# Later casts for the second expert, and other filler products on TensorE beside the first row gather

## The chip, the cores and the metric

The kernel runs on one core of a Trainium2 chip. The metric is the device time of one launch in microseconds (us). Three runs of the kernel before gave 1000.73, 1001.07 and 1002.69 us; their median is 1001.07 us. A difference is told from no change when it is over 0.2%, which is 2.0 us here.

## The reference

Attention over 48 pairs of batch and head with normalised queries and keys, then a mixture of eight experts with a fixed capacity of 224 tokens each, then one dense block with an ELU:

```python
def _moe_ref(x, w_gate, w1, w2):
    cap = N // E                      # 1792 // 8 = 224 tokens for each expert
    logits = x @ w_gate
    # tokens are given out greedily by logit, at most cap for each expert
    ...
    for e in range(E):
        mask = assigned == e
        h = np.maximum(x[mask] @ w1[e], 0.0)      # [224, 768] @ [768, 1024]
        out[mask] = h @ w2[e]                     # [224, 1024] @ [1024, 768]

def _moe2_ref(x, w_in, w_out):
    h = x @ w_in
    g = np.where(h > 0.0, h, np.exp(np.minimum(h, 0.0)) - 1.0)
    return (g @ w_out)
```

## The kernel before

The span has four parts: attention with the gate's logits (to about 300 us), the assignment of tokens to experts (to about 331 us), the eight experts (to about 570 us), and the dense block, whose second product is done by a scheme with seven products in place of eight (to the end). The change touches the seam between the assignment and the experts, from 331 us on. Experts are counted from 0 in the code, so "the second expert" is expert 1.

Every float32 operand of the experts is split into two float16 parts, a high one and a low one, and each product is the sum of three float16 products (high by high, high by low, low by high). For one expert the work is this:

- **Gather** (`Rows.gather`, line 875): two indirect DMAs, issued by GpSimd, fetch the expert's 224 rows as two halves `xg` of 112 rows. `gather(e + 2)` stands before the second products of expert `e`.
- **Columns** (`columns`, lines 906 to 924): ScalarE casts each half to float16 (`xh`, line 914), GpSimd subtracts for the low part (line 915; for expert 0 it is VectorE, in pieces of 256 columns), TensorE transposes both parts (`xt`, line 922; 24 products of 112 columns) and VectorE copies the result from PSUM to `xe` (line 923).
- **First products** (`ph`, line 951): eight tiles of 18 products, 224 columns each. For each tile ScalarE applies the ReLU and writes the high part of `h` (line 952), and VectorE the low part (line 953), which gives the PSUM bank back. Three banks serve `ph`.
- **Second products** (`py`, line 983): six tiles of 24 products; ScalarE and VectorE move each into `xc` (lines 933 and 934).
- **Weights**: SyncE loads each float32 tile into one of five staging buffers (`fw<-w`, line 810), ScalarE casts it (line 818), VectorE subtracts for the low part (line 820), and then the staging buffer is free for the next load. The first weights of expert 0 (`wa`) are made during the assignment, its second weights (`w2`, lines 802 and 806) between its `ph` tiles.

What sets the order: each engine runs its queue strictly in order. Blocks under `tc.manual_schedule()` keep the order of the code; elsewhere the order on each engine is made at build time by a scheduler that models the engines, and `tc.issue_after(x)` tells it to place instructions behind instruction `x`. The weights of expert 1 are placed behind the fourth ReLU of expert 0 in this way (`W.after`, lines 815 to 820). In the kernel before, `columns(1)` has no such condition, and the scheduler places its casts ahead of the ReLUs of expert 0 on ScalarE, and its first transposes inside the first `ph` tile on TensorE.

Between the end of the assignment and the arrival of expert 0's rows, TensorE runs 18 products into a bank nobody reads (line 940, tile `warm`). TensorE's clock has two granted levels, 1.2 and 2.4 GHz; the profile shows them as 0.50 and 1.00.

Of the kernel before, what the change touches and what calls it, by code (L numbers as in the profile page):

```python
# [20 lines left out]
P = 128  # L21
# [857 lines left out]
def moe(tc, xp, pre, xs, idx, idh, W, rows, ring, w1_d, w2_d, wi_d, wo_d, lin, g_d, t_d, out):  # L879
    nc = tc.nc  # L880
    with tc.tile_pool(name="mp", bufs=1, space=PSUM, reuse_waits="tile") as pp:
        bank = lambda t, name: pp.tile([P, 512], F32, tag=PS[t][0], name=name, bufs=PS[t][1])
# [8 lines left out]
        def wi_prep(f):  # L891

            for f in (f, f + 8):
                a = W.read64(wi_d[f], f"wi{f}")
                w = wic[f] = ring.tile([P, 2, 768], F16, tag="w1", name=f"wic{f}", bufs=8)
                nc.scalar.activation(w[:, 0], a, AF.Copy, scale=SW)
                nc.vector.scalar_tensor_tensor(w[:, 1], a, SW, w[:, 0], ALU.mult, ALU.subtract)
# [3 lines left out]
        with tc.tile_pool(name="m1", bufs=1, reuse_waits="tile") as sp:  # L901
            xe = {0: rows.first}

            def gather(e):
                xe[e] = rows.gather(e, [sp.tile([P, DM], F32, tag="xg", name=f"xg{e}_{h}", bufs=4) for h in range(2)])

            def columns(e):
                xg, x = xe[e], sp.tile([P, 6, 2, CAP], F16, tag="xe", name=f"xe{e}", bufs=2)
                hl = [sp.tile([P, 2, DM], F16, tag="xh", name=f"xh{e}_{h}", bufs=3) for h in range(2)]
                n = 256 if e == 0 else DM  # L910
                for h in (1, 0):
                    for a in range(0, DM, n):
                        x32, hi, lo = xg[h][0:112, a:a + n], hl[h][0:112, 0, a:a + n], hl[h][0:112, 1, a:a + n]
                        nc.scalar.activation(hi, x32, AF.Copy)  # L914
                        (nc.vector if e == 0 else nc.gpsimd).tensor_tensor(lo, x32, hi, ALU.subtract)  # L915
                xe[e] = x
                for d in range(0, 6, 2):
                    pt = bank(2 if e == 0 and d == 4 else 0, f"xt{e}_{d}").bitcast(F16)[:, 0:4 * CAP].rearrange("p (d j c) -> p d j c", d=2, j=2)
                    for k in range(2):
                        for h in (1, 0):  # L920
                            for j in range(2):
                                nc.tensor.transpose(pt[:, k, j, 112 * h:112 * h + 112], hl[h][0:112, j, (d + k) * P:(d + k + 1) * P], idh[0:112, 0:112])  # L922
                    last = nc.vector.tensor_copy(x[:, d:d + 2], pt)
                return last.ins

            def result(e, d, ps):

                ps = ps.rearrange("p (h c) -> p h c", h=2)
                for c, (a, b) in zip(xc, CB):
                    lo, hi = max(a, 112 * e), min(b, 112 * e + 112)  # L930
                    if lo < hi:
                        z, c = ps[:, :, lo - 112 * e:hi - 112 * e], c[:, :, d, :, lo - a:hi - a]
                        nc.scalar.activation(c[:, :, 0], z, AF.Copy, scale=SY)
                        nc.vector.scalar_tensor_tensor(c[:, :, 1], z, SY, c[:, :, 0], ALU.mult, ALU.subtract)

            with tc.manual_schedule():
                gather(1)
                warm = bank(2, "warm")
                for _ in range(18):
                    nc.tensor.matmul(warm, idh, W.ws[0].rearrange("p a b -> p (a b)")[:, 0:512], start=True, stop=True)  # L940
                W.after = columns(0)
                nc.vector.tensor_copy(ix2[0:112], idx[0:112])

                nc.scalar.dma_start(lin.rearrange("(h e r) -> r (h e)", h=2, e=E), ix2[0:112].rearrange("p h e -> p (h e)"))

                def first(e, f, w):
                    x, h = xe[e], hs[e]
                    ps = bank(1, f"ph{e}_{f}")[:, 0:CAP]
                    for d in range(6):
                        for n, (i, j) in enumerate(((0, 0), (0, 1), (1, 0))):  # L950
                            nc.tensor.matmul(ps, w[:, i, d * P:(d + 1) * P], x[:, d, j], start=d == 0 and n == 0, stop=d == 5 and n == 2)  # L951
                    relu = nc.scalar.activation(h[:, f, 0], ps, AF.Relu)
                    nc.vector.scalar_tensor_tensor(h[:, f, 1], ps, 0.0, h[:, f, 0], ALU.max, ALU.subtract)  # L953
                    return relu

                hs = {0: sp.tile([P, 8, 2, CAP], F16, tag="h", name="h0", bufs=2)}
                for f in range(8):
                    relu = first(0, f, W.ws[f])
                    if f == 3:
                        W.after = relu.ins  # L960
                    if f < 6:
                        if f >= 2:
                            W.second()
                        W.rest(f)
            nc.sync.dma_start(id2, lin.rearrange("(g p) -> p g", p=P))
            for e in range(E):
                if e:
                    hs[e] = sp.tile([P, 8, 2, CAP], F16, tag="h", name=f"h{e}", bufs=2)
                    for f in range(8):
                        first(e, f, W.split("w1", 8, w1_d[e, f], 768, f"w1_{e}_{f}"))  # L970
                h = hs[e]
                if e + 2 < E:
                    gather(e + 2)
                if e + 1 < E:
                    columns(e + 1)
                else:
                    wi_prep(0)
                for d in range(6):
                    w = W.split("w2", 6, w2_d[e, d], 1024, f"w2_{e}_{d}") if e else W.w2[d]
                    ps = bank(2, f"py{e}_{d}")[:, 0:CAP]  # L980
                    for f in range(8):
                        for n, (i, j) in enumerate(((0, 0), (0, 1), (1, 0))):
                            nc.tensor.matmul(ps, w[:, i, f * P:(f + 1) * P], h[:, f, j], start=f == 0 and n == 0, stop=f == 7 and n == 2)  # L983
                    result(e, d, ps)
        pre.close()
        with tc.tile_pool(name="wb", bufs=1, reuse_waits="tile") as wp:
# [64 lines left out]
            with tc.tile_pool(name="l1", bufs=1, side="right", reuse_waits="tile") as sp:  # L1051
# [21 lines left out]
                for f in range(8):  # L1073
# [10 lines left out]
                    if f == 7:  # L1084
                        first = operands(0, late)
# [80 lines left out]
```

## Time and profile before

| what | value |
|---|---|
| median of three runs | 1001.07 us |
| the profiled execution, its own time | 1000.04 us |
| its span, first to last instruction | 998.1 us |
| TensorE busy | 953.1 us (95%) |
| weight loads on TensorE | 629.7 us (63%) |
| VectorE busy | 754.9 us (76%) |
| ScalarE busy | 522.3 us (52%) |
| GpSimd busy | 287.1 us (29%) |
| mean granted TensorE clock | 0.985 |

The profiled execution took 1.9 us more than its span; that part lies around the program. TensorE is the busiest engine, but its share is an average: what a change at one place is worth is read from that place. Busy time of TensorE counts a product from its start to a modelled end, so products in a close row overlap in it; the distance from start to start is the price of one. "PEld" in the rows is TensorE's weight load, "SP" is SyncE, and "releaser" is what ended a wait.

### The profile page before, as it was taken

To read this page: it belongs to the slowest core of one execution; us is meant where nothing else is said; L and a number is where in the kernel's file an instruction comes from. 1 tells how busy PE (TensorE), PEld (TensorE's weight loads), DVE (VectorE), ACT (ScalarE), POOL (GpSimd) and SP (SyncE) were. 2 spreads that over 40 slices of the span, in tenths; PEclk is the share of its full clock that TensorE was granted. 3 is DMA by queue.
4 is the path that set the end of the run, shared out by engine and by line. 5 is a ranking of instruction groups with operands and counts; after the bars stand their busy time and mean duration, and the time that the engine had idled before them with its cause. 6 is when DMAs were issued, how large, how long until landed. Compare 5 with 4: busy or idle time off the path is not lost.

```text
span 998.1 us, 18586 instructions
## 1 busy us (share of the span) xinstructions
PE 953.1 (95%) x6922; PEld 629.7 (63%) x6922; DVE 754.9 (76%) x1424; ACT 522.3 (52%) x1148; POOL 287.1 (29%) x434
## 2 busy tenths in 40 slices
PE   5899999999998799999999999999999989999997
PEld 2445555555555499999999955555555546666664
DVE  6899999999958587877778699999924565555630
ACT  4778888888874276566664434334312233323330
POOL 5678888888721531121100000000000001000000
PEclk8999999999999799999999999999999999999999
DMA  9433434435215778877677168788674653333000
GB/s 336 164 104 117 127 118 123 145 115 148 56 39 177 188 205 265 263 240 225 207 236 247 38 232 266 236 284 253 209 241 122 201 151 107 100 112 115 34 32 32
DMA packets 100639, 164.92 MB, mean 165 GB/s; under 512 B 32960, under 2 KB 66240, under 8 KB 100160
## 3 DMA queue, kind: packets, MB, share of 16 engines
q1 hardware_dynamic: 96336, 152.66, 48.4%
q0 software_dynamic: 2400, 11.01, 3.6%
q8 instruction: 56, 0.92, 0.4%
q14 instruction: 39, 0.32, 0.1%
q10 hardware_dynamic: 1808, 0.01, 0.1%
HBM read 131.66 MB, written 31.99 MB: 164 GB/s over the span
## 4 chain that ended last, share of the span: by engine, by line
PE 58%; DMA 5%; DVE 1%; issue 1%; SPq 0%; ACT 0%; POOL 0%; POOLq 0%; ACTq 0%; DVEq 0%
PE l L1062 17%; PE ph L951 11%; PE py L983 11%; PE o_b L1101 10%; PE o_c L1101 6%; DMA g_d<-e 3%; PE o_a L1101 2%; PE xt L922 1%; DMA q<-g_d 1%; DMA xg<-xs,idx 1%; DVE e L1066 0%; DMA out<-xc,id 0%; DVE e L1065 0%; SPq L1022 0%; POOL xh L915 0%
## 5 line engine op out<-in xcount | busy, mean ns | idle before, releaser
L1062 PE MATMUL l<-xc,wic 128*128 128x384 f16 (+1 forms) x1152 | 218.2, 352 | 0.0
L1062 PEld LDWEIGHTS <-wic 128*128 128x128 f16 x1152 | 112.7, 98 | 104.8
L1101 PEld LDWEIGHTS <-a 128*128 128x128 f16 x1080 | 106.0, 98 | 75.3 <-ACT a L1038 3.9
L1117 POOL DMA_INDIRECT out<-xc,id x14 | 15.4, 1100 | 467.9 <-DVE xc L1110 441.8
L820 DVE SCALAR_TENSOR_TENSOR w<-fw,w 128x768 f16<-128x768 f32 (+1 forms) x98 | 110.0, 1127 | 25.9 <-ACT w L818 25.8
L244 ACT ACTIVATE p<-s,nb,r 128x448 f32<-128x448 f32 x144 | 104.0, 723 | 31.1 <-DVE nb L231 30.8
L983 PE MATMUL py<-h,w 128*128 128x224 f16 x1152 | 113.5, 259 | 0.0
L983 PEld LDWEIGHTS <-w 128*128 128x128 f16 x1152 | 109.8, 98 | 0.2
L225 DVE TENSOR_REDUCE nm<-s 128x1 f32<-128x448 f32 x168 | 102.9, 612 | 3.6 <-PE s L220 3.1
L951 PE MATMUL ph<-xe,w 128*128 128x224 f16 x1008 | 98.8, 259 | 1.4 <-DVE h L953 1.4
L951 PEld LDWEIGHTS <-w 128*128 128x128 f16 x1008 | 96.5, 98 | 1.6 <-issue 1.6
L1064 ACT ACTIVATE e<-l 128x512 f32<-128x512 f32 (+1 forms) x64 | 34.6, 541 | 113.8 <-PE l L1062 113.6
L818 ACT ACTIVATE w<-fw 128x768 f16<-128x768 f32 (+1 forms) x98 | 90.6, 928 | 5.9 <-DMA fw<-w 5.6
L282 ACT ACTIVATE e<-pt 128x448 f32<-128x448 f32 (+2 forms) x216 | 83.0, 422 | 12.3 <-PE pt L273 11.2
L297 PE MATMUL o<-e,v 128*64 128x448 f32 x384 | 87.8, 558 | 1.6 <-DVE xl L309 1.6
L273 PE MATMUL pt<-idn,p 128*128 128x128 f32 x432 | 71.4, 277 | 1.8 <-ACT p L244 1.4
L273 PEld LDWEIGHTS pt<-idn,p 128*128 128x128 f32 x432 | 50.6, 142 | 24.2 <-ACT e L282 13.2
L220 PE MATMUL s<-ks,qh 128*128 128x448 f16 x144 | 52.0, 361 | 12.5 <-ACT p L244 10.8
L915 POOL TENSOR_TENSOR xh<-xg,xh 112x768 f16<-112x768 f32 x14 | 24.3, 1755 | 129.8 <-ACT xh L914 129.8
L231 DVE TENSOR_TENSOR nb<-nm,r 128x1 f32<-128x1 f32 x168 | 59.4, 353 | 2.9
L1038 ACT ACTIVATE a<-s 128x1024 f16<-128x1024 f32 (+2 forms) x30 | 28.5, 966 | 55.8 <-PE o_b L1101 31.9
L1039 DVE SCALAR_TENSOR_TENSOR a<-s,a 128x1024 f16<-128x1024 f32 (+2 forms) x30 | 33.1, 1117 | 26.1 <-ACT a L1038 26.0
(244 smaller groups left out, 1668.0 us busy)
## 6 DMA issues: line engine op xcount, KB each, us to landing
fw<-w SPq DMA_DIRECT2D x56, 384.0 KB, 3.8
fw<-w SPq DMA_DIRECT2D x42, 512.0 KB, 4.5
xwi<-wi SPq DMA_DIRECT2D x16, 768.0 KB, 6.6
xwo<-wo SPq DMA_DIRECT2D x16, 768.0 KB, 5.1
q<-g_d SPq DMA_DIRECT2D x24, 512.0 KB, 3.7
qT<-qT SPq DMA_DIRECT2D x24, 448.0 KB, 4.2
qk<-qk SPq DMA_DIRECT2D x23, 448.0 KB, 3.5
g_d<-e SPq DMA_DIRECT2D x32, 256.0 KB, 4.4
```

Of the source, the lines that this page charges most:

```text
L225: nc.vector.tensor_reduce(d["nm", u], d["s", u][:, 0:448], AX.X, ALU.max, negate=True)
L231: nc.vector.tensor_tensor(d["nb", u], d["nm", u], d["r"][:, rc:rc + 1], ALU.mult)
L244: nc.scalar.activation(dst, d["s", u][:, 0:448], AF.Exp, bias=d["nb", u], scale=d["r"][:, rc:rc + 1], accum_out=d["sm"][:, rc:rc + 1])
L273: nc.tensor.transpose(pt[:, j * P:(j + 1) * P], p[j][:, h, 64 * h + c * P:64 * h + (c + 1) * P], idn)
L282: move = nc.vector.tensor_copy if u not in (0, 1, 2, 4, 5, 6) else lambda o, x: nc.scalar.activation(o, x, AF.Copy)
L297: nc.tensor.matmul(d["o"][64 * h:64 * h + 64, 0:448], d["v"][:, c + 4 * h, :], d["e", min(2 * c + h, 6)], start=c == 0, stop=c == 3)
L818: nc.scalar.activation(w[:, 0], f, AF.Copy, scale=SW)
L820: nc.vector.scalar_tensor_tensor(w[:, 1], f, SW, w[:, 0], ALU.mult, ALU.subtract)
L951: nc.tensor.matmul(ps, w[:, i, d * P:(d + 1) * P], x[:, d, j], start=d == 0 and n == 0, stop=d == 5 and n == 2)
L983: nc.tensor.matmul(ps, w[:, i, f * P:(f + 1) * P], h[:, f, j], start=f == 0 and n == 0, stop=f == 7 and n == 2)
L1062: nc.tensor.matmul(ps, w[:, i, d * P:(d + 1) * P], xc[cb][:, h, d, j], start=d == 0 and m == 0, stop=d == 5 and m == 2)
L1101: nc.tensor.matmul(ps, a[x][:, f, i], wt[b][f][:, j], start=first and f == 0 and k == 0, stop=f == 7 and k == 2, skip_group_check=True)
```

## The change

Two edits. The 18 filler products of 512 float16 columns become 46 others: 18 in float32 with 73 columns against 128 columns of weights, then ten pairs in float16 with 448 columns, each pair on the two halves of the array's rows (partitions 0 to 63 and 64 to 127, into two banks), then four pairs in float32 with 64 columns against 64 columns of weights on two quadrants. And `columns(1)` is placed behind the last product of the last `ph` tile of expert 0 (`mm.ins`) and behind its fifth ReLU (`relu4.ins`).

```diff
             with tc.manual_schedule():
                 gather(1)
-                warm = bank(2, "warm")
-                for _ in range(18):
-                    nc.tensor.matmul(warm, idh, W.ws[0].rearrange("p a b -> p (a b)")[:, 0:512], start=True, stop=True)
+
+                w0, w1, f0 = bank(2, "warm0"), bank(1, "warm1"), W.f2[0]
+                for k in range(18):
+                    nc.tensor.matmul(w0[:, 0:73], f0[:, k % 7 * P:(k % 7 + 1) * P], f0[:, 896:969], start=True, stop=True)
+                hl = W.ws[0].rearrange("p a b -> p (a b)")
+                for k in range(10):
+                    for r, w in ((0, w0), (64, w1)):
+                        nc.tensor.matmul(w[:, 0:448], hl[r:r + 64, k * P:(k + 1) * P], hl[r:r + 64, 0:448], start=True, stop=True)
+                for k in range(4):
+                    for r in (0, 64):
+                        nc.tensor.matmul(w0[r:r + 64, 0:64], f0[r:r + 64, k * 64:(k + 1) * 64], f0[r:r + 64, 896:960], start=True, stop=True)
                 W.after = columns(0)
...
-                            nc.tensor.matmul(ps, w[:, i, d * P:(d + 1) * P], x[:, d, j], start=d == 0 and n == 0, stop=d == 5 and n == 2)
+                            mm = nc.tensor.matmul(ps, w[:, i, d * P:(d + 1) * P], x[:, d, j], start=d == 0 and n == 0, stop=d == 5 and n == 2)
...
-                    return relu
+                    return relu, mm
...
-                    relu = first(0, f, W.ws[f])
+                    relu, mm = first(0, f, W.ws[f])
...
+                    if f == 4:
+                        relu4 = relu
...
                 if e + 1 < E:
-                    columns(e + 1)
+
+                    with ExitStack() as later:
+                        if e == 0:
+                            later.enter_context(tc.issue_after(mm.ins))
+                            later.enter_context(tc.issue_after(relu4.ins))
+                        columns(e + 1)
```

The scheduler turns this into the following moves. In the names the first number is the expert, the second the half or tile; the last is a running number. TensorE's queue inside the first `ph` tile of expert 0, before:

```order
L951 MATMUL ph0_0_6752<-xe0_6704,wa0_5076 128x224
L922 LDWEIGHTS xh1_1_6942
L922 MATMUL xt1_0_6947<-idh_68,xh1_1_6942 128x112
L951 LDWEIGHTS wa0_5076
L951 MATMUL ph0_0_6752<-xe0_6704,wa0_5076 128x224
```

TensorE's queue behind the last `ph` tile of expert 0, now:

```order
L959 LDWEIGHTS wa7_5424
L959 MATMUL ph0_7_6942<-xe0_6733,wa7_5424 128x224
L922 LDWEIGHTS xh1_1_6971
L922 MATMUL xt1_0_6976<-idh_68,xh1_1_6971 128x112
L922 LDWEIGHTS xh1_0_6970
L922 MATMUL xt1_0_6976<-idh_68,xh1_0_6970 128x112
```

The transposes of expert 1 stood after six, and again after twelve, of the first tile's 18 products, and now the first of them stand behind the eighth tile; part of the `py` products of expert 0 stands ahead of that tile, before and now.

ScalarE's queue between the rows of expert 0 and its first ReLUs, before:

```order
L914 ACTIVATE xh0_0_6705<-xg0_0_4993 112x256 x3
L914 ACTIVATE xh1_1_6942<-xg1_1_6682 112x768
L914 ACTIVATE xh1_0_6941<-xg1_0_6681 112x768
L914 ACTIVATE xh2_1_7354<-xg2_1_6937 112x768
L944 DMA lin_65<-ix2_6672 112x16x1
L952 ACTIVATE h0_6751<-ph0_0_6752 128x224
```

ScalarE's queue from the fifth ReLU of expert 0 on, now:

```order
L960 ACTIVATE h0_6780<-ph0_4_6873 128x224
L802 ACTIVATE w2_0_4_6894<-b4_5005 128x1024
L914 ACTIVATE xh1_1_6971<-xg1_1_6682 112x768
L914 ACTIVATE xh1_0_6970<-xg1_0_6681 112x768
L818 ACTIVATE w1_1_4_7275<-fw1_1_4_7273 128x768
L914 ACTIVATE xh2_1_7383<-xg2_1_6966 112x768
L960 ACTIVATE h0_6780<-ph0_5_6897 128x224
```

The two casts of expert 1 and the first cast of expert 2 leave the place ahead of the ReLUs and now stand on both sides of a weight cast, ahead of the sixth ReLU.

GpSimd's queue at the subtractions of expert 1, now:

```order
L915 TENSOR_TENSOR xh1_1_6971<-xg1_1_6682,xh1_1_6971 112x768
L915 TENSOR_TENSOR xh1_0_6970<-xg1_0_6681,xh1_0_6970 112x768
L875 DMA xg3_1_7378<-xs_63,idx_70 112x768
L915 TENSOR_TENSOR xh2_1_7383<-xg2_1_6966,xh2_1_7383 112x768
L875 DMA xg3_0_7377<-xs_63,idx_70 112x768
```

Before, the first gather of expert 3 stood between the two subtractions of expert 1; now it stands behind both. SyncE's queue has the same order before and now.

## Rows read from the trace of the kernel before

**Rows 1.** The page's first line.

```profile
span 998.1 us, 18586 instructions
```

**Rows 2.** TensorE's waits after 338 us: total, times, longest.

```profile
PE xt L922 <- ACT xh L914: 3.5, 1, 3.5
...
PE xt L922 <- POOL xh L915: 1.4, 1, 1.4
```

**Rows 3.** The chain that ended last, 334 to 400 us: start, us, what.

```profile
335.06 7.14 DMA xg<-xs,idx
...
346.60 12.49 PE ph L951 x114
...
370.24 2.40 PE ph L951 x25
```

**Rows 4.** Stretches: us, engines busy, granted clock, DMA share, GB/s.

```profile
331.00:336.00 5.00, 4.55 (x11) 1.61 (x12) 1.79 (x5) 0.73 (x3) 2.23 (x2) 0.50 0.80 226
336.00:339.00 3.00, 3.00 (x34) 2.05 (x33) 2.71 (x8) 1.33 (x4) 2.39 (x3) 0.99 0.93 312
...
343.00:346.00 3.00, 1.44 (x8) 1.06 (x9) 0.00 (x0) 1.46 (x3) 2.56 (x2) 0.50 0.58 161
...
386.00:800.00 414.00, 414.00 (x3248) 306.90 (x3247) 326.51 (x521) 181.06 (x308) 22.65 (x14) 1.00 0.69 221
807.00:810.00 3.00, 2.37 (x8) 1.04 (x8) 3.00 (x5) 3.00 (x6) 0.00 (x0) 0.51 0.00 0
```

**Rows 5.** The timeline, 326 to 350 us: start, us, engine, line, tiles, shape, count.

```profile
331.45 6.30 PE L940 MATMUL warm<-wa,idh 128*128 128x512 f16 x18 [1.51 <-PEq L702]
...
337.58 1.34 PE L922 MATMUL xt<-idh,xh 112*128 112x112 f16 x24
...
338.86 0.73 PE L951 MATMUL ph<-xe,wa 128*128 128x224 f16 x6
...
345.05 0.93 POOL L875 DMA_INDIRECT xg<-xs,idx  x1 [0.27 <-POOL xh L915]
```

**Rows 6.** TensorE's groups by shape, whole span: count, busy us, mean ns.

```profile
L1062 PE MATMUL l<-xc,wic 128*128 128x512 f16 x576 | 125.8, 379 | 0.0
```

**Rows 7.** Float32 weight loads by shape, whole span: count, busy us, mean ns.

```profile
L297 PEld LDWEIGHTS o<-e,v 128*64 128x64 f32 x384 | 21.3, 135 | 22.8 <-issue 16.8 <-DVE xl L309 3.3 <-DVE nb L231 1.0
L271 PEld LDWEIGHTS pt<-idn,pTl 128*128 128x128 f32 x72 | 10.2, 141 | 11.6 <-issue 7.2 <-DVE e L290 0.9 <-POOL pTl L255 0.7
...
L543 PEld LDWEIGHTS st<-LL,ones 128*128 128x128 f32 x2 | 0.3, 191 | 0.0
```

**Rows 8.** Timeline of weight loads near 24 us, clock granted 0.50.

```profile
24.86 0.23 PEld L271 LDWEIGHTS pt<-idn,pTl 128*128 128x128 f32 x1
```

**Rows 9.** Timeline of TensorE near 205 us, two column halves in float32.

```profile
205.33 0.97 PE L297 MATMUL o<-e,v 128*64 128x448 f32 x4 [0.20 <-DVE xl L309]
```

**Rows 10.** Timeline of TensorE near 279 us, one float32 product.

```profile
279.50 0.41 PE L543 MATMUL st<-LL,ones 128*128 128x144 f32 x2
```

**Rows 11.** Timeline, 344 to 372 us.

```profile
365.47 1.56 ACT L914 ACTIVATE xh<-xg 112x768 f16<-112x768 f32 x2
366.37 4.27 POOL L915 TENSOR_TENSOR xh<-xg,xh 112x768 f16<-112x768 f32 x2 [13.15 <-ACT xh L914]
...
367.57 1.58 DVE L820 SCALAR_TENSOR_TENSOR w<-fw,w 128x768 f16<-128x768 f32 x1
...
369.90 0.36 ACT L933 ACTIVATE xc<-py 128x224 f16<-128x224 f32 x1 [2.87 <-PE py L983]
```

**Rows 12.** Timeline, 372 to 400 us.

```profile
385.60 0.95 DVE L820 SCALAR_TENSOR_TENSOR w<-fw,w 128x768 f16<-128x768 f32 x1
385.74 5.33 PE L951 MATMUL ph<-xe,w 128*128 128x224 f16 x54 [1.45 <-DVE h L953]
```

**Rows 13.** ScalarE's waits, 355 to 385 us: total, times, longest.

```profile
ACT w L818 <- DMA fw<-w: 4.8, 3, 3.5
```

**Rows 14.** The gathers of line 875, all 16.

```profile
DMA to landing us min/median/max: 4.6/7.0/12.0
```

## The prediction

> **What bounds the kernel now.** I read the page first: the span is 998.1 us [rows 1], and the profiled execution took 1000.04 us, 1.03 below the median of the runs shown. I work in this execution's own time and take the gain off the median. Next the waits of TensorE behind 338 us [rows 2]: there are two of 3.5 and 1.4 us, on ScalarE's and GpSimd's parts of the rows that TensorE transposes, and one of 1.45 us later, on VectorE's part of `h` [rows 12]. The chain [rows 3] tells whose rows they are: before the two waits it runs through a gather issued at 335.06 that took 7.14 us to land, which is the second expert's. Its casts and transposes stand in front of the first expert's products, for which all was there. Third, the stretches [rows 4]: the granted clock is 0.50 from 331 to 336, 0.99 from 336 to 339, and 0.50 again from 343 to 346, after TensorE had stood still. From 386 to 800 TensorE is busy 414.00 of 414.00 us, so whatever is won before 386 and still there at 386 is kept: after it, TensorE itself is the bound and no supplier was late.
>
> **What goes.** The first expert's 126 `ph` products of its first seven tiles start at 338.86 [rows 5] and end at 346.60 + 12.49 = 359.09 [rows 3]: 20.2 us. At the high level 25 of them take 2.40 us [rows 3], 0.096 each, so 126 take 12.1. The difference of 8.1 is the two waits (4.9), six transposes that sit between, and the stretch at the low level behind the waits. With `columns(1)` behind the fifth ReLU and the last tile, nothing in front of these products reads the second expert's rows, so all 8.1 goes, if the clock stays up. What could be late next is ScalarE's and VectorE's work for each tile; its order is unchanged, and TensorE never waited for it among these products [rows 2], most of which ran at full speed. ScalarE's store of the index list (line 944), which stood behind the three casts, is issued earlier, and SyncE, whose weight loads stand behind a load that waits for it, is freed no later.
>
> **What the new filler costs.** The old filler ran from 331.45 to 337.75 and the transposes began at 337.58 [rows 5]: it was over just when the rows were ready. The new one has three parts.
>
> First, 18 float32 products. One such product is two passes: the row for line 543 shows two for one product, 0.41 us together and 0.29 for one alone, so 0.12 from start to start for 144 columns [rows 10]; 73 columns stream in 0.062 at the high level. But each pass loads 128 columns of float32 weights. A load of 64 columns is 135 ns and one of 128 is 191 [rows 7]; the 56 ns between them are 64 columns, so 128 take 0.112 and a pass is limited by its load. At the low level a float32 load took 0.23 against 0.141 [rows 7, 8], 0.09 more where the columns' own share is smaller than here, so I double it: 0.22 a pass. No trace shows such passes in a row, so the bounds are 0.062 (0.124 low) and 0.112 (0.22 low), and I take the load's, since the row for its size exists.
>
> Second, ten pairs on row halves. 512 float16 columns cost 125.8/576 = 0.218 [rows 6], so 448 cost 0.19, and 0.38 at the low level. No row has row halves; the nearest has column halves: four float32 passes of 448 columns, each 0.37 by the price above, end within 0.97 us [rows 9], where one after another they would need over 1.49. Two ran at a time. I take the same for row halves: 1.9 us for ten pairs, with 3.8 as the other end.
>
> Third, four pairs of float32 quadrants: 16 passes of 64 columns, 0.056 each by the load, two at a time: 0.45.
>
> The clock decides the rest. In the kernel before it rose at 336, after the filler had run without a gap from 331.45 at the low level [rows 4, 5]. Passes limited by their loads leave no gap either, and I expect the same rise. Then 4.6 us at 0.22 are 21 passes; the other 15 take 1.7, to 337.7; the pairs end at 339.6, the quadrants at 340.1. Then 24 transposes, 1.34 [rows 5], and `ph` starts at 341.4 instead of 338.86. So 2.6 of the 8.1 is given back and the first seven tiles end 5.5 earlier.
>
> In the Trainium skill, TensorE: Matmul & The Clock Gate, section LDWEIGHTS, a weight load takes its columns divided by 1.2 GHz, whatever the array's level: 107 ns for 128 columns. At the high level that agrees with the 0.112 from the rows; at the low level it would leave a pass at the 0.124 of its stream, which is the rival of the short filler below. The low-level load of 0.23 [rows 8] speaks against it.
>
> **What comes back behind it.** I follow the queues on the time line of before, all shifted by the same 5.5. On ScalarE three casts (0.8 each, two in 1.56 [rows 11]) move behind the fifth ReLU: 2.4 us, of which 1.3 fall into waits for weights that end there now (4.8 in three waits, less the longest of 3.5 [rows 13]). On VectorE two copies of 0.6 move behind the last ReLUs, and three subtractions of GpSimd now run beside weight splits: such a split took 1.58 beside one [rows 11] and 0.95 alone [rows 12], 0.6 each. So the last eight transposes of the second expert end near 369.5, where before the casts behind them began at 365.47 [rows 11]. The cast for the third expert writes a buffer that these still read, and behind it stands a cast that needs the fourth expert's rows. Their gather is issued at 345.05 now [rows 5]; behind both subtractions it will be near 364, and the median gather takes 7.0 [rows 14], so these two casts end near 372.2 instead of 367.0, and the first `xc` cast comes 2.4 later than its 369.90. TensorE itself loses about 0.3 there. But the weights behind that cast give their staging buffers back later, their loads follow, and the 1.45 wait at 385.74 [rows 12], which hangs on such a load, ends 1.3 to 2.1 later, counting 0.6 for products that the new order puts behind it. I take 1.7. The ends are 0.3, if the loads have room, and 5, if that gather takes the 12.0 us of the slowest.
>
> **The sum.** 8.1 − 2.6 − 1.7 = 3.8 us less: 996.2 for the profiled execution, 997.3 against the median. The later wait at 807 with its stretch at the low level [rows 4] moves along; whether its idle time again lets the clock fall is worth 1.4 either way.
>
> **The rivals.**
> *Short filler.* Float32 passes limited by their stream: 36 × 0.124 = 4.5, done at 335.9; pairs to 337.9, quadrants 338.3, transposes 339.7, which is 1.7 earlier: 995.6. For it: streams are what set float16 prices. Against: the 191 ns load.
> *Low clock.* The clock doesn't rise during the float32 part, since no row shows it rise on passes that wait for their loads: 36 × 0.22 = 7.9, to 339.4; the pairs run at the low level, 3.8, to 343.2, and lift it; quadrants 343.6, transposes 345.0. That is 3.6 later: 1000.9, no change. For it: from 343 to 346 the engine worked 1.44 of 3 us and the clock stayed at 0.50 [rows 4].
> *Filler too long (slower).* Low clock, and row halves one after another: 339.4, then half of the pairs at the low level (3.8) and half at the high one (1.9), 345.1, quadrants 345.5, transposes 346.9, 5.5 later: 1002.8; 1006.5 if the level stays low to the transposes' end (20 × 0.38, 0.9, 2.7 in place of 3.8 + 1.9, 0.45, 1.34). The point from which it decides is a `ph` start at 345.2, a filler that ends past 343.9. For it: no row shows row halves side by side. Against: column halves do run so.
> *The change doesn't do what it says.* Excluded by the order: no instruction ahead of the fifth ReLU reads the second expert's rows.
>
> **How the numbers follow.** Forecast (the sum) 0.42, short filler 0.12, low clock 0.30, too long 0.16. The likeliest case has its own range of 995.9 to 999.0: the 0.3 behind it, and half of the way to the 5. The whole range, 995.2 to 1002.8, leaves out the best part of the short filler and half of the longest. Faster by over 0.2% is below 999.07: nearly all of the forecast (0.40), the short filler (0.12) and a little of low clock (0.03), 0.55. Slower is above 1003.07: half of too long (0.08) and 0.02 of low clock, 0.10. Within is 0.35.
>
> **What would show it.** In the profile of the changed kernel: no wait of TensorE on `xh` between the first transposes and the `py` products, and 126 `ph` products in 12.1 us at clock 1.00; the 36 float32 passes, 0.22 and then 0.11 from start to start; ten pairs starting two by two; `ph` at 341.4; the fourth expert's gather issued near 358 (364 less the shift) with ScalarE waiting for it; and the wait for `h` still there, longer by about a microsecond. I am wrong if the clock is at 0.50 past 337, if row halves start one stream apart, or if the wait near 380 has grown by as much as the start has moved.

## The result, and the profile after

The changed kernel took 1006.52 us (ten runs, 1004.68 to 1010.51) beside 1001.03 for the kernel before: a ratio of 1.0056, 95% interval 1.0043 to 1.0069. It is slower by 5.5 us; the forecast was 3.8 faster. The profiled execution took 1007.35, its span is 1005.4.

The page's first line, and TensorE's waits behind 330 us (total, times, longest), of the changed kernel. The experts' first products are now line 959, the filler is lines 941, 945 and 948, and the second layer of the dense block is line 1116:

```profile
span 1005.4 us, 18696 instructions
```

```profile
PE o_c L1116 <- ACT a L1053: 5.6, 1, 5.6
PE xt L922 <- DVE xe L923: 2.7, 1, 2.7
PE warm L941 <- PEq L702: 2.4, 1, 2.4
PE ph L959 <- DVE h L961: 1.7, 1, 1.7
...
PE xt L922 <- POOL xh L915: 0.3, 1, 0.3
```

The waits of 3.5 and 1.4 us on `xh` [rows 2] are gone; a wait of 2.7 on VectorE's copy `xe` is new, and the last wait, 3.5 before, is 5.6.

TensorE's timeline of the changed kernel around the filler (start, us, engine, line, tiles, shape, count), and its stretches (us, then busy us and count of PE, PEld, DVE, ACT, POOL, granted clock, DMA share, GB/s):

```profile
332.23 7.93 PE L941 MATMUL warm<-b 128*128 128x73 f32 x36 [2.41 <-PEq L702]
340.09 3.92 PE L945 MATMUL warm<-wa 64*128 64x448 f16 x20
343.93 0.70 PE L948 MATMUL warm<-b 64*64 64x64 f32 x16
344.57 1.35 PE L922 MATMUL xt<-idh,xh 112*128 112x112 f16 x24
345.86 1.31 PE L959 MATMUL ph<-xe,wa 128*128 128x224 f16 x12
```

```profile
331.00:336.00 5.00, 3.77 (x18) 3.80 (x19) 2.24 (x6) 1.03 (x3) 2.40 (x2) 0.50 0.82 251
336.00:340.00 4.00, 4.00 (x20) 3.95 (x19) 1.54 (x5) 1.03 (x3) 3.05 (x4) 0.50 0.90 279
340.00:344.00 4.00, 4.00 (x23) 1.43 (x24) 0.00 (x0) 0.00 (x0) 0.00 (x0) 0.50 1.02 263
346.00:358.00 12.00, 12.00 (x127) 12.00 (x126) 9.62 (x14) 7.06 (x12) 0.00 (x0) 1.00 0.20 9
...
386.00:800.00 414.00, 412.32 (x3250) 306.86 (x3248) 329.45 (x527) 185.01 (x318) 22.81 (x14) 1.00 0.69 220
812.00:818.00 6.00, 4.44 (x14) 1.89 (x15) 4.77 (x8) 5.75 (x10) 0.00 (x0) 0.50 0.01 3
```

TensorE was busy from 336 to 339 in both kernels, but the clock that stood at 0.99 there [rows 4] is at 0.50 until 344. `ph` starts at 345.86 instead of 338.86 [rows 5]. Then 126 products run in 12 us at clock 1.00 without a wait, and the first `py` product comes at 357.93 (before: 359.43). So at that point the change is 1.5 us ahead. Expert 2's first product is 4.5 us behind (410.25 against 405.75), and all stays at 4.5 until the second layer of the dense block, whose second tile is 7.3 behind. Behind that point the loss is made in two places that the forecast priced at 1.7 and at nothing (1.4 either way).

The first of them, the changed kernel's timeline from 359 to 371:

```profile
359.19 5.05 POOL L915 TENSOR_TENSOR xh<-xg,xh 112x768 f16<-112x768 f32 x2 [19.23 <-ACT xh L914]
...
360.61 2.13 DVE L820 SCALAR_TENSOR_TENSOR w<-fw,w 128x768 f16<-128x768 f32 x1 [0.18 <-ACT w L818]
...
362.96 2.37 DVE L806 SCALAR_TENSOR_TENSOR w<-b,w 128x1024 f16<-128x1024 f32 x1
...
364.39 1.75 POOL L875 DMA_INDIRECT xg<-xs,idx  x1
...
365.55 3.96 DVE L820 SCALAR_TENSOR_TENSOR w<-fw,w 128x768 f16<-128x768 f32 x2
...
369.44 0.61 DVE L923 COPY xe<-xt 128x896 f16<-128x896 f16 x1
...
370.10 0.55 PE L922 MATMUL xt<-idh,xh 112*128 112x112 f16 x8 [2.74 <-DVE xe L923]
...
370.64 0.84 ACT L914 ACTIVATE xh<-xg 112x768 f16<-112x768 f32 x1 [5.45 <-issue]
```

Beside GpSimd's subtractions, which now lie here, a split of VectorE takes 2.13 and 2.37 us where it takes 0.95 [rows 12] and about 1.2 alone. The copy for which TensorE waits stands behind them in VectorE's queue. The splits also give the staging buffers back late, and expert 2's first weights reach ScalarE at 384.18; 379.79 before. One row of each kernel, of after and of before:

```profile
384.18 0.84 ACT L818 ACTIVATE w<-fw 128x768 f16<-128x768 f32 x1 [4.00 <-DMA fw<-w]
```

```profile
379.79 0.84 ACT L818 ACTIVATE w<-fw 128x768 f16<-128x768 f32 x1 [3.51 <-DMA fw<-w]
```

This cast is 4.4 us later, and expert 2's first product 4.5: it comes 26.1 us behind the cast here and 26.0 in the kernel before, and 23.5 to 27.7 in all the traces below.

### The profile page after: what moved, and what is told of

Read it like the earlier page. It is cut to its first block, busy times and chain, and to the rows that moved or that the text cites. A ratio compares the mean times of both kernels' runs of the same rounds, so it can differ in the third digit from the quotient of the medians.

```text
span 1005.4 us, 18696 instructions
## 1 busy us (share of the span) xinstructions
PE 960.2 (95%) x6976; PEld 637.2 (63%) x6976; DVE 759.1 (76%) x1424; ACT 521.6 (52%) x1148; POOL 287.6 (29%) x434
## 4 chain that ended last, share of the span: by engine, by line
PE 58%; DMA 3%; DVE 1%; ACT 1%; issue 0%; SPq 0%; POOLq 0%; ACTq 0%; DVEq 0%
PE l L1077 21%; PE o_b L1116 10%; PE py L998 10%; PE ph L959 9%; PE o_c L1116 6%; PE o_a L1116 2%; DMA g_d<-e 1%; DMA fw<-w 1%; PE xt L922 1%; DVE w L820 0%; ACT w L818 0%; DMA out<-xc,id 0%; SPq L1037 0%; POOLq L1178 0%; DVE xc L934 0%
## 5 line engine op out<-in xcount | busy, mean ns | idle before, releaser
L820 DVE SCALAR_TENSOR_TENSOR w<-fw,w 128x768 f16<-128x768 f32 (+1 forms) x98 | 113.0, 1156 | 27.5 <-ACT w L818 27.5
L1116 PE MATMUL o_b<-wb,a 128*128 128x384 f16 x312 | 52.7, 326 | 0.0
```

Source lines behind the costliest of these rows:

```text
L820: nc.vector.scalar_tensor_tensor(w[:, 1], f, SW, w[:, 0], ALU.mult, ALU.subtract)
L1116: nc.tensor.matmul(ps, a[x][:, f, i], wt[b][f][:, j], start=first and f == 0 and k == 0, stop=f == 7 and k == 2, skip_group_check=True)
```

## The experiments

Each ran against the kernel before on the same chip. In the table: the start of three products against the trace of before (us; expert 0's first, expert 2's first, the second tile of the second layer, from one trace each), the median, and the ratio with its 95% interval. The two traces of the changed kernel differ by 1.4 at expert 2 and by 3.2 at layer 2, so smaller differences there between two runs tell little.

| run | expert 0 | expert 2 | layer 2 | median | ratio |
|---|---|---|---|---|---|
| changed kernel | +7.0 | +4.5 | +7.3 | 1006.52 | 1.0056 [1.0043, 1.0069] |
| e12 changed again | +6.6 | +3.1 | +4.1 | 1005.57 | 1.0050 [1.0032, 1.0068] |
| e1 new filler, old place | +6.8 | +0.6 | +4.5 | 1002.83 | 1.0025 [1.0008, 1.0042] |
| e2 old filler, new place | +0.7 | -0.4 | -1.0 | 998.76 | 0.9984 [0.9971, 0.9996] |
| e3 float16 for float32 | +0.8 | +0.3 | +2.1 | 1002.11 | 1.0024 [1.0009, 1.0039] |
| e4 no float32 products | 0.0 | -2.9 | -3.7 | 998.66 | 0.9992 [0.9977, 1.0007] |
| e11 wide float32 | +6.4 | +3.6 | +4.9 | 1006.05 | 1.0052 [1.0033, 1.0071] |
| e5 subtractions on VectorE | +7.1 | +3.3 | +5.0 | 1004.72 | 1.0034 [1.0020, 1.0049] |
| e6 copies on ScalarE | +6.8 | +3.8 | +6.7 | 1007.14 | 1.0058 [1.0043, 1.0072] |
| e9 six buffers | +6.2 | +3.2 | +5.9 | 1005.79 | 1.0055 [1.0033, 1.0076] |
| e13 no gathers 3 to 7 | +6.2 | +3.0 | +6.1 | 1004.01 | 1.0030 [1.0018, 1.0042] |
| e14 e13, subtractions 1, 2 on VectorE | +5.9 | -1.5 | +1.7 | 1000.36 | 0.9994 [0.9983, 1.0005] |
| e15 before, no gathers 3 to 7 | +0.2 | -3.4 | -5.0 | 996.85 | 0.9969 [0.9957, 0.9981] |
| e7 e4, subtractions 1 on VectorE | +0.1 | -4.3 | -3.9 | 998.21 | 0.9977 [0.9966, 0.9988] |
| e8 e4, copies on ScalarE | +1.0 | -3.6 | -2.4 | 997.68 | 0.9979 [0.9964, 0.9995] |
| e16 e4, subtractions 1, 2 on VectorE | +0.3 | +1.0 | +0.6 | 998.77 | 0.9984 [0.9973, 0.9995] |
| e10 e7, six buffers | 0.0 | -4.2 | -3.3 | 996.45 | 0.9959 [0.9943, 0.9975] |
| e17 before, 72 filler products | +1.0 | +0.7 | +1.0 | 1003.69 | 1.0030 [1.0018, 1.0043] |
| e18 before, e10's other edits | +6.2 | +0.7 | -0.1 | 1002.44 | 1.0010 [1.0000, 1.0021] |

**The two halves of the change, e1 and e2.** In e1 the place of `columns(1)` is that of before; in e2 the filler is.

```diff
-        w0, w1, f0 = ...   # e2: the three new loops out, the old loop back
+        for _ in range(18): nc.tensor.matmul(warm, idh, ...[:, 0:512], ...)
```

> The new filler alone; expert 1's casts and transposes stay where the kernel before has them. Theory A (the filler's first part keeps the clock low, so that the filler costs 7 us, and the move itself gains): first product of expert 0 at 345.9 us, clock up at 344 as in the changed kernel; of the two waits on xh (3.5 and 1.4 us) little is left, since the gather has had 7 us more: 1001 + 7.0 - 4.9 = 1003.1 us. Rival B (the loss is behind expert 0, made by the move): the 7 us are taken back at the xh waits and the low stretch behind them, 1000 to 1001.5 us.

> The move alone; the old filler of 18 float16 products of 512 columns. Theory A: first product of expert 0 at 338.9, first product of the second layer at about 351 (12.1 us of products without a wait), and the stretch behind costs what it did in the changed kernel: 1006.5 - 7.0 = 999.5 us. Rival B (behind expert 0 it is the gather, the loads and the splits that set the time): the 7 us come back as waits of TensorE on xh, xe or the weights between 350 and 410, expert 2's first product stays at about 410, and the time at 1004 to 1006.5 us.

e1 took the time of A by way of B. The filler starts expert 0 6.8 us late, but the waits on `xh` take nearly all of that up (no such wait is left in its trace), and expert 2 is 0.6 behind; the rest of its 2.5 us comes at the second layer. e2 took A's time too, but again B's mechanism is in it: its first `py` product is 7.8 us ahead of before, and expert 2 only 0.4. TensorE's waits of e2 behind 338 us:

```profile
PE ph L952 <- DVE h L954: 3.3, 1, 3.3
PE o_c L1109 <- ACT a L1046: 3.1, 1, 3.1
PE xt L922 <- DVE xe L923: 2.7, 1, 2.7
```

So the parts do not add. The filler costs 2.5 us in the old place and 6.9 in the new one (1.0053, the mean of two measurements, less 0.9984); the move gains 1.6 with the old filler and loses 2.8 with the new one. The waits for expert 1's rows were also the cover under which a long filler was nearly free (0.6 at expert 2). Not all of these costs belong to the filler's length: e17 below has the old filler columns in as many products as the new filler, and costs 3.0 in the old place.

**The filler's clock, e3, e4 and e11.** Of the float32 loop

```diff
-for k in range(18): nc.tensor.matmul(w0[:, 0:73], f0[:, k % 7 * P:(k % 7 + 1) * P], f0[:, 896:969], ...)
+for k in range(36): nc.tensor.matmul(w0[:, 0:73], hl[:, k % 7 * P:(k % 7 + 1) * P], hl[:, 896:969], ...)    # e3
+for k in range(9): nc.tensor.matmul(w0[:, 0:512], f0[:, k % 7 * P:(k % 7 + 1) * P], f0[:, 0:512], ...)     # e11
```

and in e4 nothing stands in its place.

> As changed, but the 18 float32 products (two passes each) are 36 float16 products of the same 73 columns, each with a weight load of its own. Theory A1 (it is the float32 operands that leave the clock low): clock up at about 336.5, 36 x 0.11 = 3.9 us for the first part, ph0 at about 340, 1001 us. Theory A2 (few columns behind a full weight load leave it low, whatever the type): the first part takes 36 x 0.11 low = 3.9 us, clock up 7 us behind the first pair, at 343, pairs at the low level, ph0 at about 342, 1002.5 us. Rival B: 1004 us or more, since the loss is behind.

> As changed without the 18 float32 products: ten pairs of row halves and the quadrants alone. Theory A: pairs from 332.2, 3.8 us at the low level, quadrants to 336.6, transposes behind xh at about 337.4, ph0 at about 339, clock up between 336 and 340, 999.5 us. Rival A3 (row halves do not raise the clock either): the clock stays low through the first products of expert 0, ph0 at 339 to 340, 126 products at 0.19 instead of 0.096 for some 7 us: 1003 us. Rival B (loss behind): 1004 to 1006.5 us.

> As changed, but the 18 float32 products of 73 columns are 9 of 512 columns: the same type and weights, about the same 7.7 us (18 passes of 0.43 us at the low level, the float16 pass of 512 columns). Theory A2 (it is the short passes behind full weight loads, in which the array stands idle most of the time, that leave the clock low): clock up at about 336 to 337 as before, the rest of the filler at the high level, ph0 at 341.5 to 342.5, and 1.5 to 3 us less than the changed kernel where behind expert 0 nothing else bounds: 1004 us. Theory A1 (float32 operands leave it low): clock up at 344, ph0 at 345.9, 1006.5 us.

The timeline of TensorE in e3, then in e11, and the stretches of e11:

```profile
331.27 2.38 PE L942 MATMUL warm<-wa 128*128 128x73 f16 x36 [1.07 <-PEq L702]
333.58 1.67 PE L945 MATMUL warm<-wa 64*128 64x448 f16 x7
336.31 1.48 PE L945 MATMUL warm<-wa 64*128 64x448 f16 x13 [1.05 <-issue]
```

```profile
331.84 9.54 PE L941 MATMUL warm<-b 128*128 128x512 f32 x18 [1.58 <-PEq L702]
```

```profile
331.00:335.00 4.00, 3.16 (x4) 1.50 (x5) 0.86 (x2) 0.00 (x0) 0.86 (x1) 0.50 0.86 260
335.00:341.00 6.00, 6.00 (x15) 2.47 (x13) 2.84 (x8) 1.95 (x6) 4.21 (x4) 1.00 0.78 257
```

With 512 columns behind the same float32 weights the clock is up from 335, so the type does not hold it down (A1 falls); with 73 columns it stayed low until 344 in the changed kernel. In e3 the float16 passes took 0.061 each, not the 0.11 expected, the pairs came 1.6 us earlier than assumed, and the clock rose at 335 with them; which of the two lifted it e3 doesn't tell. In e4 it rose at 335.8 on pairs and quadrants. A2 is right on the clock and wrong on the time: the wide passes are 0.86 us at the low level and 0.43 at the high one, twice a float16 pass, so that part alone is 9.5 us long in place of 7.9, `ph` starts at 345.21, and 1006.05 us is no gain. Without float32 products 6.1 us of the changed kernel's time are gone (1.0053 to 0.9992). That is not only a filler that ends earlier: e3 starts expert 0 within 0.1 us of e2 and expert 2 within 0.7, yet it lies at 1.0024 and e2 at 0.9984, and at the second layer the two are 3.0 apart. e3 has 6976 products on TensorE, as the changed kernel (a float32 one counts twice), e2 6922 and e4 6940; e17 takes this up.

**What comes back, e5 and e6.** They take the wait on `xe` away in two ways:

```diff
-(nc.vector if e == 0 else nc.gpsimd).tensor_tensor(lo, x32, hi, ALU.subtract)
+(nc.vector if e <= 1 else nc.gpsimd).tensor_tensor(lo, x32, hi, ALU.subtract)     # e5
-last = nc.vector.tensor_copy(x[:, d:d + 2], pt)
+nc.scalar.activation(x[:, d:d + 2], pt, AF.Copy)     # e6, for e == 1
```

> As changed, but the two subtractions of expert 1's rows run on VectorE instead of GpSimd. Theory S (the splits on VectorE are stretched beside GpSimd's subtractions, 2.13, 2.37 and 3.96 for two in place of 0.95, 1.22 and 1.9, some 4.4 us in all, and so the copy for which TensorE waits 2.7 us is late): VectorE has 2.2 us more of its own (from 0.37 for 256 columns), the splits go back to 0.95 and 1.22, the wait on xe falls from 2.7 to about 0.5, the low stretch of the clock at 371 goes, expert 2's first product at about 407 to 408 instead of 410.25, 1003 us. Rival Q (VectorE's queue is long by itself): the wait stays at 2 to 3 us, 1006 us.

> As changed, but the three copies of expert 1's transposed rows run on ScalarE, which stood idle for 5.45 us there. Theory C (TensorE's 2.7 us are the copy's place in VectorE's queue): the copy ends by about 364.5, the wait on xe and the low stretch at 371 are gone, expert 2's first product at about 406 to 407, 1002.5 us. Rival L (behind it the weights' splits, still stretched, are as late as the copy): TensorE waits for w on VectorE instead, expert 2's first product at 409 or later, 1005.5 us.

TensorE's waits from 338 to 800 us, of e5 and of e6:

```profile
PE ph L959 <- DVE h L961: 2.7, 1, 2.7
PE xt L922 <- DVE xe L923: 0.4, 1, 0.4
```

```profile
PE ph L962 <- DVE h L964: 2.3, 1, 2.3
PE py L1001 <- DVE h L964: 1.7, 1, 1.7
```

The wait on `xe` goes, and a longer one on `h` takes its place; expert 2 stays 3.3 and 3.8 behind, within the 3.1 to 4.5 that two traces of the changed kernel show. e5 is some 2 us lower (1.0034), with an interval that overlaps theirs, and e6 gains nothing. C falls; L has the place of expert 2 right, though TensorE waits for `h` and not for the weights. S is right on the wait on `xe` and wrong on expert 2 (409.06). The copy was not what bound: the cast of expert 2's first weights starts at 383.53 in e5 and at 384.01 in e6, hardly earlier than the 384.18 of the changed kernel. e5 leaves expert 2's subtractions on GpSimd, and splits beside them stay long.

**Are they the gathers? e9, e12 to e15.** In the kernel before three gathers lie between 345 and 352 (the first at 345.05 [rows 5]), in the changed kernel five between 364 and 378, beside the weight loads.

```diff
-tag="xg", name=f"xg{e}_{h}", bufs=4    # e9: bufs=6
+if e >= 3:                             # e13, e14 (with "e <= 2" in the line of e5), e15
+    xe[e] = raw[e] = raw[e - 2]
+    return
```

> As changed, with six row buffers in place of four, so that the gather of expert 3 (two DMAs) doesn't wait for expert 1's casts and subtractions and is issued beside expert 2's. Theory G (the move pushes the gathers into the stretch in which the weights are loaded, 364 to 384 us; they share the DMA queues' engines, and the load for which ScalarE waits 4.0 us lands at 384.1): two of five gathers leave that stretch, the load of w_2_0 lands about 2 us earlier, the wait on h goes from 1.7 to near 0, expert 2's first product at 408 to 408.5, 1004.5 us. Rival S (only the stretched splits and the copy count): the load lands earlier, the wait on xe stays at 2.7, expert 2's first product at 410, 1006 us.

> The changed kernel once more, for a second trace of it. What comes from the change is there again: ph0 at about 345.9, the clock up at 344, the wait on xe of 2.7, expert 2's first product 4.5 us later than before. If the wait on a at the second layer (5.6 us against 3.5) comes from DMAs that land differently in each run, it is another here (3 to 7 us); if it belongs to the change, it is 5.6 again.

> The changed kernel without the gathers of experts 3 to 7 (they take the rows of experts 1 and 2 again). Theory G (the gathers hold the loads up): no gather lies beside the loads from 364 on, the load of w_2_0 is in flight for about 4 us instead of 6.7 and lands at about 381, expert 2's first product 1.5 to 2.5 us behind the kernel before instead of 3.1 to 4.5. Theory S (the stretched splits hold the buffers): it is still issued 21 us behind the first load; expert 2's first product stays at 3 or more.

> As the run without the gathers of experts 3 to 7, and the subtractions of experts 1 and 2 on VectorE. Theory S and G together: the load of w_2_0 is issued 17 to 18 us behind the first one, as before the change, is in flight for 4 us, and lands at 378 to 379; expert 2's first product within 1 us of the kernel before (406 to 407). If a third thing holds it, the product stays 2 us or more behind.

> The kernel before without the gathers of experts 3 to 7 (they take the rows of experts 1 and 2 again): what the gathers cost there. By G three of the five lie in the quiet stretch between 345 and 352, and two beside the loads: w_2_0 lands up to 1 us earlier, 1000 to 1001 us. If it falls by 2 us or more, the gathers cost as much before the change as behind it, and G explains nothing of the difference.

e9 tested nothing: two gathers left the stretch, the next experts' took their place, and its loads, counted from the first, are issued to a tenth as in e12. e12 puts the changed kernel's loss at expert 2 at 3.1 to 4.5. In e13 it is 3.0, the least that S allows, and in e14 the cast starts where S and G together put it, with expert 2 even 1.5 ahead. The splits from 355 to 376 us by shape (count, busy us, mean ns), of after and of e14, and e14's row of expert 2's first weights:

```profile
L820 DVE SCALAR_TENSOR_TENSOR w<-fw,w 128x768 f16<-128x768 f32 x8 | 10.6, 1364 | 0.2 <-ACT w L818 0.2
L806 DVE SCALAR_TENSOR_TENSOR w<-b,w 128x1024 f16<-128x1024 f32 x3 | 4.8, 1602 | 0.2 <-ACT w L802 0.2
L820 DVE SCALAR_TENSOR_TENSOR w<-fw,w 128x1024 f16<-128x1024 f32 x1 | 2.5, 2489 | 0.6 <-ACT w L818 0.6
```

```profile
L820 DVE SCALAR_TENSOR_TENSOR w<-fw,w 128x768 f16<-128x768 f32 x8 | 7.3, 946 | 0.0
L820 DVE SCALAR_TENSOR_TENSOR w<-fw,w 128x1024 f16<-128x1024 f32 x4 | 4.8, 1207 | 0.0
```

```profile
378.87 0.84 ACT L818 ACTIVATE w<-fw 128x768 f16<-128x768 f32 x1 [3.08 <-DMA fw<-w]
```

and SyncE's waits for splits (total, times, longest), 340 to 392 us, in before and in after:

```profile
SPq L810 <- DVE w L820: 10.4, 8, 2.2
```

```profile
SPq L810 <- DVE w L820: 12.4, 8, 5.5
```

That load was issued 16.2 us behind the first one in the kernel before, 21.0 in the changed kernel, 19.1 in e5, 20.0 in e13, 18.4 in e14 and 16.5 in e15. In flight it was for 5.8 us in the kernel before, 6.7 in the changed kernel and 5.3 in e13, not the 4 that G asked for; so most of its delay is its issue. Without the gathers the changed kernel gains 2.0 to 2.6 us (1.0030), but the kernel before gains 3.1 (0.9969): by the criterion set for e15, G explains nothing of the difference. Without gathers on either side, the change costs 6.1 us with the subtractions on GpSimd and 2.5 with those of experts 1 and 2 on VectorE (0.9994). So taking the subtractions from GpSimd is worth 3.6 of the 6.1 there, net of what they cost VectorE. Whether it would gain as much in the kernel before without gathers was not run, so that these 3.6 belong to the change is argued, not shown; and of the 3.5 us by which e13 issues that load later than e15, e14 takes back 1.6. With the gathers in place e5 recovered only about 2; how the two work on each other was not taken further.

**A version that beats both, e7, e8, e10, e16 and e18.** These build on e4.

> The changed kernel without the float32 products, and expert 1's subtractions on VectorE. Theory S: the variant without float32 products had 998.7 us, and 2 to 4 us of the stretch behind expert 0 go: 995 to 996.5 us. Rival Q: 998 to 999 us. Rival D (there the loads and gathers are next: 5 us earlier and still expert 2 not before 403): 998 us.

> The changed kernel without the float32 products, and expert 1's copies on ScalarE. Theory C: 998.7 - 2.7 - some of the low stretch = 995 to 996 us. Rival L or D (weights, loads or gathers are next): 998 us.

> The changed kernel without float32 products, with expert 1's subtractions on VectorE and six row buffers. By theories S and G together 1.5 to 2 us below the variant without the buffers (998.2): 996 to 996.7 us, no wait of over 1 us on h at expert 1. Rival (nothing is bound by the gathers there): 998 us.

> The changed kernel without float32 products, with the subtractions of experts 1 and 2 on VectorE. Theory S: no split stands beside GpSimd between 350 and 375, so another 0.5 to 1.5 us below the variant with expert 1's alone (998.2): 997 us. Rival: VectorE's own 3.6 us for four subtractions push its copies and splits back by as much: 999 us.

> The kernel before with expert 1's subtractions on VectorE and six row buffers; neither filler nor place is changed. If the best variant (996.45 us, ratio 0.9959) gains by the move and the shorter filler, this one is at 999.5 to 1001 us, since the xh waits of 3.5 and 1.4 us (for ScalarE's casts and the gather) stay. If subtractions and buffers alone do it, 996.5 to 998 us.

e10 is the best: 996.45 us, 0.41% below the kernel before (0.25 to 0.57). Its edits without the move and the shorter filler (e18) gain nothing. But e18 is no plain control: in the old place the subtraction of expert 1 stands ahead of expert 0's copies in VectorE's queue, and TensorE waits 6.2 us for `xe` where the kernel before waits 3.5 and 1.4 for `xh`. e7 and e8 came out at 998.21 and 997.68, above what S and C forecast and near D; their intervals overlap those of e4 and e10, so single edits aren't told apart. e16 has the rival's time but not its mechanism: its wait of 6.8 us on `h` follows a load that was issued at 369.5, as early as in e7, and landed 10.2 us later (8.2 in e7), and VectorE stood idle for 7.6 us until that weight's cast; why the load took so long is open.

**The second layer, e17.**

```diff
-for _ in range(18): nc.tensor.matmul(warm, idh, ...[:, 0:512], ...)
+for _ in range(72): nc.tensor.matmul(warm[:, 0:128], idh, ...[:, 0:128], ...)
```

> The kernel before, its 18 filler products of 512 columns cut into 72 of 128 (the same columns; 6976 matrix products, as many as the changed kernel has). Theory F (the place of an instruction transfer among the loads of q delays the second layer): the transfer lies 3 to 4 us behind the layer's first product, the wait on a is 4.5 to 7 us, the layer is 1 to 4 us later, 1002 to 1003 us. Rival (the wait has to do with the move or the float32 products): expert 2's first product within 0.7 us of before, the wait on a 2.5 to 4, 1000.7 us.

The wait on `a` at the second layer in e12 and in e17:

```profile
PE o_c L1116 <- ACT a L1053: 4.5, 1, 4.5
```

```profile
PE o_c L1101 <- ACT a L1038: 3.4, 1, 3.4
```

The same kernel has 5.6 and 4.5 in two traces, so part of it differs from run to run. e17's median is 3 us above before though nothing but the number of filler products, for the same columns, is new: that the number costs is shown. Where it costs is not. e17's one trace is the shortest of its twelve runs: the transfer (16 KB of instructions, 2.9 us behind the layer's first product) lies where F wants it, and the wait is 3.4. The other traces fit F. In the nine others with 6976 products the transfer lies 3.1 to 4.0 us behind the layer's first product, and the wait is 4.5 to 7.1; in the ten with fewer products the nearest one lies over 8 us away, and the wait is 2.1 to 3.9. No run moves the transfer alone, so this part of the cause is argued from 19 of 20 traces and stays open.

## Why the prediction was wrong

- **What goes, 8.1 us: right.** From the first `ph` to the first `py` product it is 12.07 us instead of 20.6, and no wait on `xh` lies between. e2 shows it by itself: 7.8 us at the first `py`.
- **A float32 pass limited by its load, 0.22 low: right, and partly by luck.** 36 took 7.93 us, with weight loads busy for 3.95 of 4.00. The working took the group at 191 ns for a load of 128 columns and passed over the one at 141 [rows 7], which would have made 64 columns 6 ns. The formula of the Trainium skill, TensorE: Matmul & The Clock Gate, section LDWEIGHTS, names neither a type nor a clock level; the estimate by it is 107 ns for 128 columns. For these float32 loads at the low level it falls, since it leaves no more than 0.124 for such a pass. With it falls the short filler.
- **Row halves two at a time: right.** Ten pairs took 3.9 us at the low level, 0.37 a pair; with it falls "filler too long" as it was priced.
- **"Passes limited by their loads leave no gap either, and I expect the same rise": this step failed.** The clock rose at 344, not at 336, and `ph` started at 345.86, not 341.4: the filler cost 7.0, not 2.6. A clock at 0.50 past 337 was a sign of being wrong that the prediction had named. That is the rival "low clock" for the filler itself (3.6 later than forecast, and 0.8 more by a later start). The sentence took TensorE's busy time for the thing that lifts the clock; the stretch with clock 0.50 and 4.00 of 4.00 us busy refutes it.
- **What comes back, 1.7 us: mis-sized.** It is about 5: from 1.5 ahead to 4.5 behind, less 1 for the 16 transposes that now stand behind the products. With the old filler (e2) it is 7.4 of the 7.8. In the trace it is the 2.7 on `xe`, 0.3 on `xh`, 0.2 more on `h`, and 1.7 for a stretch at the low level from 371.3 to 374.7, behind TensorE's standstill. I had priced three splits beside GpSimd at 0.6 more each; there are four, at 1.2 to 2.1 more (2.13, 2.37, 3.09 and 2.49 us), and I let them push the copies but not the buffers, and so not the loads by that path. The path through expert 3's gather was wrong: the gather landed at 369.07, and the casts that were to wait for it began at 370.64, when the last transposes, behind the copy, had started. e14 against e13 shows the subtractions' place worth 3.6 us; the rest of the load's delay is open.
- **The sum of independent terms: wrong too.** By e1, the filler in the old place would have cost 2.5. The forecast moved the waits away and charged the filler on top of that, which is right; but it then shifted all that follows by the 5.5 left over, and the suppliers behind expert 0 did not shift with it: e2 arrives 7.8 early and has 0.4 of it left at expert 2. A price for 54 more products was not in the sum at all; e17 measures 3.0 for it.
- **The wait at 807, "worth 1.4 either way":** 2.8 in the profiled execution, 1.1 in the second trace; open.

Rival "filler too long (slower)" has the measured time at the end of its range, 1002.8 to 1006.5, but not its mechanism. The start that it names, `ph` past 345.2, came; by the prediction's own sum a start at 345.86 gives 1001.8, and the other 4.7 us come from behind expert 0 and from the second layer.

## What to carry to other kernels

A wait is also cover: before it is removed, list what was free under it (here a filler of 7 us and the subtractions and gathers of the next expert), and price each of them where it lies afterwards. A step that is moved takes along everything that hangs on its outputs, on every queue; look at what those instructions will stand beside, not only at what they stand behind. Judge a filler by when it ends and by how many instructions it adds, and don't take busy time alone as a sign that the clock will rise.

## What the runs showed of the hardware

- A float32 pass of 73 columns behind a weight load of 128 columns takes 0.22 us at the low level, a float16 pass of the same size 0.061; of 512 columns a float32 pass takes 0.86 at the low and 0.43 at the high level. With the first, TensorE was busy without a gap for 7.9 us (332.2 to 340.1) and the clock stayed at 0.50; it rose at 344.0, behind 3.9 us of row-half pairs. With the wide passes it was up after 3.2 us.
- VectorE's splits and GpSimd's subtractions stretch each other: 2.13 us for 0.95 on the one side, 5.05 for two on the other, where one takes 1.63 beside an idle VectorE (at 343.15 in the kernel before). The Trainium skill, SBUF — State Buffer, section Who interferes with whom, says that a VectorE instruction with two SBUF inputs contends with a GpSimd instruction that reads SBUF; the trace agrees: with the subtractions of experts 1 and 2 on VectorE (e14) the splits are at 0.95 and 1.21.
- The same 9216 filler columns in 72 products instead of 18 cost 3 us in the median, of which the one trace, of the fastest run, shows 1.0.
